# Causal attention with a cumulative bias, then two feed-forward layers: the last 64 queries of two heads in one score tile

## The chip, the cores and the metric

The kernel runs on one core of one Trainium2 chip. The metric is the device time of one execution in microseconds (us); three timed executions of the kernel before gave 1062.91, 1063.27 and 1064.26 us, the median being 1063.27 us. TensorE (PE) multiplies matrices into PSUM, VectorE (DVE), ScalarE (ACT) and GpSimd (POOL) do the elementwise work, and SyncE (SP) issues the DMAs.

## The reference

```python
# q, k, v: (4, 8, 576, 64), s: (4, 8, 576)
scores = (1/sqrt(64)) * q @ k.T
cum = cumsum(max(s, 0), axis=-1)
scores = where(causal, -1e9, scores + min(-(cum_i - cum_j), 0))
attn = softmax(scores)                      # rows of 576
x = (attn @ v)                              # to (2304, 512): heads side by side
x = sigmoid(x @ w_gate) * (x @ w_val) @ w_out          # 512 -> 1536 -> 512
h = x @ w_in;  out = (h - tanh(h)) @ w_out2            # 512 -> 2048 -> 512
```

Per row of scores the term with cum_i alone cancels in the softmax, so the kernel adds only a per-key term.

## The kernel before, in words

**Stages.** Four stages follow each other: attention together with the first feed-forward layer's gate and value products (to about 484 us), the rest of these products, the product with w_out, and the second layer. The change touches the first stage alone. Most operands are kept as two fp32r halves, a high and a low one (x = xh + xl, made by ACT as a rounding copy and by POOL or DVE as a subtraction), so that a product takes two or three fp32r matmuls.

**Units and steps.** A unit is one head of one batch and one query group: group 0 has queries 0 to 255, group 1 has queries 256 to 575 with all 576 keys. All 32 units of group 0 come first, then the 32 of group 1. A unit is walked in steps, one for a tile of 128 queries (`steps`, L258): t = 0, 1 in group 0 and t = 2, 3, 4 in group 1, with 384, 512 and 576 keys. The tile t = 4 is queries 448 to 575, of which t = 3 has done the first 64 already; the scores are made for all 128, and only rows 64 to 127 are transposed and kept (L423 to L428).

**One iteration of the loop** (L612 to L695) is a software pipeline written out by hand; each engine gets its instructions in this order. In iteration i: DVE adds 1e-9 to the sum of step i-1 (`eps`), makes the biased scores and row minima of step i out of PSUM (`ttr`, L391), takes the reciprocal for step i-1 and, for t = 2, also normalises it (`norm`, L416); for t = 3 and 4 POOL normalises (L414). ACT copies the transposed probabilities of step i-2 out of PSUM and DVE makes their low halves (`evac`, L446 and L447); ACT does the exponentials of step i (L398); POOL masks the diagonal block of the bias row to be used two steps later (`mask`, L349). Then come the finishing of a head's output (`xsum` L494 and L495, in the next iteration `xsplit` L503 and L504), the tanh or gating of the feed-forward group before (`moe_post`), and one entry of `parts`: the splitting of a coming head's keys (ACT L318, POOL L319), queries (ACT L322, POOL L323) or values (L336, L337). PE's order in iteration i is: scores of step i+1 (`qk`), one feed-forward group of 12 matmuls (`moe`), the transposes of step i-1 (`tr`, into PSUM bank 6), after a head's last step the product with v (`pv`, bank 7), and further feed-forward groups.

**How many feed-forward groups** an iteration gets is k = ceil(groups waiting / iterations left), with `left` set when a batch of heads begins (L617). When the last head of a batch is finished, 24 groups for the 24 products of that batch and group are queued. In the 24 iterations of a batch one group each is the rule; in each later batch the iteration in which a new queue is filled has k = 0 (the old one is just used up), and in the middle two batches the one behind it has k = 2. The first batch of group 1 works on what group 0 left, with 256 columns a matmul; later ones have 320.

**Names.** The probabilities of one head lie in `pth`, `ptl` (one buffer, five key blocks by 320 queries); `cbc` is the bias row of a head, loaded as a broadcast over 128 partitions; `sp` is the score tile; `kh`, `kl`, `qs` are the split keys and queries; `xp`, `xh`, `xl` a pair of heads' output and its halves.

Of the kernel before, what the change touches and what calls it, by code (L numbers as in the profile page):

```python
# [25 lines left out]
MASK = -(2.0 ** 33)  # L26
CO = {0: 0, 1: 128, 2: 0, 3: 384, 4: 896}
CW = 1184
LN = 1
# [34 lines left out]
def attention_moe_moe2(ctx: ExitStack, tc: tile.TileContext, kqT, v, s, wg, wv, wo, win, wo2, out):  # L64
# [181 lines left out]
    a_right = ExitStack()  # L246
    pt = a_right.enter_context(tc.tile_pool(name="pt", bufs=1, side="right"))
# [3 lines left out]
    cv = a_right.enter_context(tc.tile_pool(name="cv", bufs=2, side="right"))  # L251

    make_identity(nc, ident)
    NPT = 1
    pts = [[]]
# [24 lines left out]
    def load_vc(u):  # L280
        if u >= len(units):
            return
        b, h, q0, kw, qw, nj = shape(u)
        d = U_[u]
        if u >= N32:
            d["v"] = ld.tile([128, 5, D], F, tag="v", name="vraw")[:, :nj]
        else:
# [20 lines left out]
    def split_kq(u):  # L308
        if u < N32 or u >= len(units):
            return  # L310
        b, h, q0, kw, qw, nj = shape(u)
        d = U_[u]
        d["kh"] = kh = at.tile([128, S], R, tag="kh", name="kh", bufs=NK)[:, :kw]
        d["kl"] = kl = at.tile([128, S], R, tag="kl", name="kl", bufs=NK)[:, :kw]
        d["qs"] = qs = at.tile([128, 320], R, tag="qs", name="qs", bufs=NK)[:, :qw]

        def part_k():
            ACT.activation(out=kh, in_=d["k"], func=AF.Copy)  # L318
            POOL.tensor_tensor(out=kl, in0=d["k"], in1=kh.bitcast(F), op=ALU.subtract)  # L319

        def part_q():
            ACT.activation(out=qs, in_=d["q"], func=AF.Copy)  # L322
            POOL.tensor_tensor(out=qs[64:128], in0=d["q"][64:128], in1=qs[64:128].bitcast(F), op=ALU.subtract)  # L323
# [20 lines left out]
    def mask(i):  # L344
        if 2 * N32 <= i < len(steps):
            u, t = steps[i]
            e = CO[t] + (288 if t == 4 else width(t))
            c = U_[u]["c"][:, e - 128:e]
            POOL.affine_select(out=c, in_=c, pattern=[[-1, 128]], base=0, channel_multiplier=1,  # L349
                               compare_op=ALU.is_ge, fill=MASK)  # L350

    def qk(i):
# [7 lines left out]
        if u < N32:  # L360
# [5 lines left out]
            return  # L366
        cuts = [(0, max(w, 256))] if t < 4 else [(0, 288), (288, 576)]
        T_[i] = {"qk": []}
        for c0, c1 in cuts:
            ps = bank(3 + nqk[0] % 3, [128, c1 - c0])  # L370
            nqk[0] += 1
            PE.matmul(ps, d["qs"][:, o:o + 128], d["kh"][:, c0:c1], start=True, stop=False)  # L372
            PE.matmul(ps, d["qs"][:, o:o + 128], d["kl"][:, c0:c1], start=False, stop=True)
            T_[i]["qk"].append((ps, c0, min(c1, w)))

    def ttr(i):
# [10 lines left out]
        for k, (ps, c0, c1) in enumerate(e.pop("qk")):  # L387
            init, acc = acc, e["nm"][:, k:k + 1]
            o = CO[t] if t < 4 else CO[4] - 288 if c0 else CO[3]
            cum_t = zero[:, 0:w] if u < N32 else U_[u]["c"][:, o + c0:o + c1]  # L390
            DVE.tensor_tensor_reduce(out=sp[:, c0:c1], in0=ps[:, 0:c1 - c0], in1=cum_t, scale=-0.125,  # L391
# [26 lines left out]
    def tr(i):  # L418
# [3 lines left out]
        e = T_[i]  # L422
        p0 = 64 if t == 4 else 0  # L423
        e["n"] = n = 128 - p0
        blocks = [128 * j for j in range(t + 1)] if t < 4 else [0, 128, 256, 384, 448]
        ps = bank(2 if i < TR2 and i % 2 else 6, [128, len(blocks), n])
        for j, c in enumerate(blocks):
            PE.transpose(ps[:, j, :], e["sp"][p0:128, c:c + 128], ident[p0:128, p0:128])  # L428
        e["tr"] = ps

    def evac(i):
# [4 lines left out]
        e = T_.pop(i)  # L436
        n = e["n"]
        if u < N32:
            if t == 0:
                U_[u]["p"] = at.tile([128, 3, 128], F, tag="vs", name="p32")  # L440
            ACT.activation(out=U_[u]["p"][:, t:2 * t + 1], in_=e["tr"], func=AF.Copy)
            return
        ph, pl = pts[u % NPT]
        o = Q0[t] - GRP[G][0] + (64 if t == 4 else 0)
        js = slice(0, t + 1) if G else slice(0, 3 * t + 1, 3)
        ACT.activation(out=ph[:, js, o:o + n], in_=e["tr"], func=AF.Copy)  # L446
        DVE.tensor_tensor(out=pl[:, js, o:o + n], in0=e["tr"], in1=ph[:, js, o:o + n].bitcast(F), op=ALU.subtract)  # L447

# [3 lines left out]
    def pv(u):  # L452
# [4 lines left out]
        if u < N32:  # L457
# [4 lines left out]
            return ps  # L462
        ph, pl = pts[u % NPT]
        jobs = [(0, 0, 0), (1, 3, 0)] if G == 0 else [(0, 0, 0), (1, 1, 0), (2, 2, 0), (3, 3, 64), (4, 4, 64)]
# [88 lines left out]
    for u in range(2):  # L553
# [5 lines left out]
    identb, upper = consts[:, 256:320].bitcast(BF), consts[:, 320:384].bitcast(BF)  # L559
    some = consts[:, 1024:1152].bitcast(BF)  # L560
    DVE.memset(zt, 0.0)
    DVE.memset(consts[:, 512:768], 0.37)
    DVE.tensor_tensor_scan(out=consts[:, 768:1024], data0=consts[:, 512:768], data1=consts[:, 512:768], initial=0.0,
                           op0=ALU.add, op1=ALU.add)
    ACT.activation(out=some, in_=consts[:, 768:1024], func=AF.Copy)
    POOL.memset(consts[:, 0:512], 0.0)
# [37 lines left out]
    lag = [2 if j < 2 * N32 else LN for j in range(n)]  # L604
    xq, xs = [], []

# [4 lines left out]

    for i in range(n + LN + 1):  # L612
# [25 lines left out]
        if i < n:  # L638
            exp(i)
            mask(i + 2)  # L640
        while xs:
            xu = xs.pop(0)
# [5 lines left out]
        while xq:  # L648
# [4 lines left out]
            else:  # L653
                xs.append(xu)
        if first:
            if vparts:
                vparts.pop(0)()
            split_kq(u + KA)
            split_v(u + 1)
# [19 lines left out]
        for e in es:  # L679
            if e == n - 1 or steps[e][0] != steps[e + 1][0]:  # L680
                xq.append((steps[e][0], pv(steps[e][0])))
        if i < n and t == 4 and vparts:
            vparts.pop(0)()
        for j in range(1, k):
# [3 lines left out]
        if i == 2 * N32:  # L688
            cvt.finish(len(cq) - 1)
            for p in "hl":  # L690
                pts[0].append(pt.tile([128, 5, 320], R, tag=f"pt{p}", name=f"pt{p}0"))
                POOL.memset(pts[0][-1][:, 3].bitcast(F), 0.0)
        if 2 * N32 + 4 <= i < 2 * N32 + 8:
            p, c = divmod(i - 2 * N32 - 4, 2)
            POOL.memset(pts[0][p][:, 3 * c + 1:c + 3 + c].bitcast(F), 0.0)  # L695
    for x in xq:
# [308 lines left out]
```

## Time and profile before

| | us |
|---|---|
| median of three timed executions | 1063.27 |
| the profiled execution, timed | 1064.41 |
| its span, first to last instruction | 1062.3 |
| PE busy (share of the span) | 1031.9 (97%) |
| DVE busy | 662.1 (62%) |
| ACT busy | 524.9 (49%) |
| POOL busy | 465.4 (44%) |

The span leaves 2.1 us of the profiled execution's time outside. Busy shares are averages over stages that differ; a matmul's row is longer than its slot on PE, as matmuls are pipelined, so the slots are read from where the next one starts. "Idle before" names what ended an engine's idle time. The granted clock is 1.00 where TensorE runs at 2.4 GHz and 0.50 where it runs at 1.2 GHz.

### The profile page before, as it was taken

The page shows a single profiled execution, that of the slowest core. Times are in us where ns is not written, and L with a number is a line of the kernel's source. Part 1 is how long each engine was busy: PE and PEld are TensorE (multiplying, and loading weights), DVE is VectorE, ACT ScalarE, POOL GpSimd, SP SyncE. Part 2 cuts the span into 40 slices and gives each one's busy share as a digit, 9 for nine tenths or more (in the row PEclk, how much of TensorE's full clock was granted, in tenths as well). Part 3 has the DMA queues.
Part 4 walks back from the last instruction along what each step waited for, and adds up shares of the span by engine and source line. Part 5 has one row for each costly group of instructions (what it writes and reads, how often), then busy time and mean ns, then how long its engine had stood idle before and what let it go on. Part 6 is the DMA issues. An engine that isn't in the chain of part 4 may idle for free.

```text
span 1062.3 us, 20117 instructions
## 1 busy us (share of the span) xinstructions
PE 1031.9 (97%) x6892; PEld 954.2 (90%) x6892; DVE 662.1 (62%) x1563; ACT 524.9 (49%) x1193; POOL 465.4 (44%) x606
## 2 busy tenths in 40 slices
PE   7888999999999999999999999999999999999998
PEld 5787999998999999999988888988888889999997
DVE  6686566777677777665523443265655245888875
ACT  6775566766666566653523333244443333334333
POOL 4676455667566666642400010046465212454442
PEclk9999999999999999999999999999999999999999
DMA  7774456757664565515553342256597687444433
GB/s 210 219 243 107 113 139 177 200 155 171 144 174 135 159 173 159 134 51 188 172 173 117 120 117 78 99 183 221 202 326 283 222 312 259 139 117 142 142 99 100
DMA packets 111142, 177.12 MB, mean 167 GB/s; under 512 B 16000, under 2 KB 75392, under 8 KB 109760
## 3 DMA queue, kind: packets, MB, share of 16 engines
q1 hardware_dynamic: 111040, 175.85, 54.6%
q8 instruction: 54, 0.88, 0.4%
q14 instruction: 48, 0.39, 0.1%
HBM read 128.79 MB, written 47.00 MB: 165 GB/s over the span
## 4 chain that ended last, share of the span: by engine, by line
PE 86%; DVE 5%; issue 3%; DMA 2%; ACT 2%; POOL 1%; SPq 1%; DVEq 0%; POOLq 0%; ACTq 0%
PE bank L526 8%; PE bank L527 8%; PE bank L530 8%; PE bank L819 6%; PE bank L818 6%; PE bank L822 6%; PE bank L958 5%; PE bank L957 5%; PE bank L956 5%; PE bank L467 5%; PE bank L777 5%; PE bank L776 5%; PE bank L780 5%; PE bank L428 4%; PE bank L372 2%
## 5 line engine op out<-in xcount | busy, mean ns | idle before, releaser
L958 PE MATMUL bank<-wo,sl 128*128 128x256 f32 x504 | 142.5, 283 | 0.8 <-DVE sl L867 0.8
L956 PE MATMUL bank<-wo,sh 128*128 128x256 f32 x504 | 141.8, 281 | 0.3 <-ACT sh L865 0.3
L957 PE MATMUL bank<-wo,sh 128*128 128x256 f32 x504 | 141.7, 281 | 0.0
L446 ACT ACTIVATE pth<-bank 128x512 fp32r<-128x512 f32 (+2 forms) x128 | 59.5, 465 | 143.4 <-PE bank L467 84.0
L819 PE MATMUL bank<-y,ring 128*128 128x512 f32 (+1 forms) x320 | 115.8, 368 | 0.0
L818 PE MATMUL bank<-y,ring 128*128 128x512 f32 (+1 forms) x320 | 115.7, 368 | 0.0
L447 DVE TENSOR_TENSOR ptl<-bank,pth 128x512 fp32r<-128x512 f32 (+2 forms) x128 | 66.7, 521 | 67.9 <-ACT pth L446 38.5
L825 DVE TENSOR_TENSOR th<-bank,th 128x512 f32<-128x512 f32 (+1 forms) x80 | 50.2, 635 | 92.6 <-ACT th L824 90.5
L114 POOL TENSOR_TENSOR ring<-tmp,ring 128x512 fp32r<-128x512 f32 x16 | 22.5, 1406 | 187.6 <-ACT ring L124 167.4
L398 ACT ACTIVATE sp<-sp,nm 128x576 f32<-128x576 f32 (+2 forms) x160 | 95.6, 597 | 7.4 <-DVE nm L391 7.4
L958 PEld LDWEIGHTS bank<-wo,sl 128*128 128x128 f32 x504 | 95.2, 189 | 1.8 <-DVE sl L867 1.2
L862 POOL TENSOR_TENSOR s<-g 128x256 f32<-128x256 f32 (+1 forms) x40 | 34.3, 858 | 141.4 <-DMA g<-h 133.8
L956 PEld LDWEIGHTS bank<-wo,sh 128*128 128x128 f32 x504 | 95.2, 189 | 0.5 <-ACT sh L865 0.5
L957 PEld LDWEIGHTS bank<-wo,sh 128*128 128x128 f32 x504 | 95.2, 189 | 0.0
L733 DVE TENSOR_TENSOR gl<-g,gh 128x512 fp32r<-128x512 f32 (+1 forms) x60 | 37.8, 637 | 84.5 <-PE bank L780 63.5
L428 PE MATMUL bank<-ident,sp 128*128 128x128 f32 (+1 forms) x480 | 74.1, 262 | 16.5 <-POOL sp L414 7.2
L824 ACT ACTIVATE th<-bank 128x512 f32<-128x512 f32 (+1 forms) x80 | 43.7, 551 | 80.4 <-PE bank L822 76.3
L732 ACT ACTIVATE gh<-g 128x512 fp32r<-128x512 f32 (+1 forms) x60 | 35.1, 591 | 90.2 <-PE bank L777 83.3
L822 PE MATMUL bank<-y,ring 128*128 128x512 f32 (+1 forms) x320 | 78.7, 368 | 0.0
L414 POOL TENSOR_SCALAR sp<-sp,r 128x512 f32<-128x512 f32 (+1 forms) x90 | 57.1, 635 | 47.3 <-DVE r L407 40.7
L428 PEld LDWEIGHTS bank<-ident,sp 128*128 128x128 f32 (+1 forms) x480 | 51.7, 139 | 28.4 <-POOL sp L414 11.1
L865 ACT ACTIVATE sh<-g 128x768 fp32r<-128x768 f32 (+1 forms) x40 | 31.3, 781 | 88.4 <-PE bank L957 58.4
(376 smaller groups left out, 3199.5 us busy)
## 6 DMA issues: line engine op xcount, KB each, us to landing
h<-th SPq DMA_DIRECT2D x64, 256.0 KB, 2.8
kq<-in_kq SPq DMA_DIRECT2D x32, 448.0 KB, 3.8
raw<-in_wo SPq DMA_DIRECT2D x28, 512.0 KB, 5.2
g<-g SPq DMA_DIRECT2D x48, 256.0 KB, 2.7
g<-h SPq DMA_DIRECT2D x72, 128.0 KB, 2.2
w<-wst SPq DMA_DIRECT2D x5, 1792.0 KB, 6.0
wo<-w SPq DMA_DIRECT2D x5, 1792.0 KB, 9.1
cbc<-cum SPq DMA_DIRECT2D x32, 256.0 KB, 5.4
```

The costliest lines, as they stand in the source:

```text
L398: ACT.activation(out=e["sp"], in_=e["sp"], func=AF.Exp, scale=-1.0, bias=e["m"], accum_out=e["sum"])
L428: PE.transpose(ps[:, j, :], e["sp"][p0:128, c:c + 128], ident[p0:128, p0:128])
L447: DVE.tensor_tensor(out=pl[:, js, o:o + n], in0=e["tr"], in1=ph[:, js, o:o + n].bitcast(F), op=ALU.subtract)
L526: PE.matmul(ps, wh[:, c], xh[:, k], start=(k == 0), stop=False)
L527: PE.matmul(ps, wl[:, c], xh[:, k], start=False, stop=False)
L530: PE.matmul(ps, wh[:, c], xl[:, k], start=False, stop=(k == KD - 1))
L818: PE.matmul(ps, wh[:, c], yh[k], start=(k == 0), stop=False)
L819: PE.matmul(ps, wl[:, c], yh[k], start=False, stop=False)
L822: PE.matmul(ps, wh[:, c], yl[k], start=False, stop=(k == KD - 1))
L956: PE.matmul(o, sh[:, g, c], w[:, 0, f], start=(p == 0 and t == 0), stop=False)
L957: PE.matmul(o, sh[:, g, c], w[:, 1, f], start=False, stop=False)
L958: PE.matmul(o, sl[:, g, c], w[:, 0, f], start=False, stop=(p == MP - 1 and t == nt - 1))
```

## The change

Heads are taken in pairs in group 1. The even head has the steps t = 2, 3 and the odd head t = 2, 3, 4: five steps a pair. The one t = 4 step holds the last 64 queries of the even head in rows 0 to 63 of its score tile and those of the odd head in rows 64 to 127. For that the split queries `qs` get 64 columns of zeros, behind the even head's last 64 queries and ahead of the odd head's, and four matmuls per half of the keys accumulate into one PSUM tile. The bias of that tile is a row of its own, `c4`, with one head in each half of the partitions. The five key blocks are transposed whole (128 by 128), four into bank 6 and the fifth into one of the banks of the scores. The probabilities are held for two heads; the two products with v stand in consecutive iterations. The splits of keys, queries and values, and the loads, are spread anew over the five iterations. The odd head's queries are split in two pieces.

```diff
@@ constants, steps
-CO = {0: 0, 1: 128, 2: 0, 3: 384, 4: 896}
-CW = 1184
+CO = {0: 0, 1: 128, 2: 0, 3: 384}
+CW = 896
-    steps = [(u, t) for u, (b, G, h) in enumerate(units) for t in GRP[G][2]]
+    steps = [(u, t) for u, (b, G, h) in enumerate(units) for t in GRP[G][2] if t < 4 or h % 2]
@@ split_kq, split_v
+        if not Q_:
+            for j in range(4):
+                Q_.append(at.tile([128, 384], R, tag="qs", name=f"qs{j}", bufs=4))
+                POOL.memset(Q_[j][:, 320 - 64 * (j % 2):384 - 64 * (j % 2)].bitcast(F), 0.0)
+        d["qs"] = qs = Q_[u % 4]
+        pieces = ((0, 256, 0), (256, 320, 320)) if qw > 256 and h % 2 else ((0, qw, 0),)
...
-        vparts.append(part_v)
+        (vparts if qw == 256 else parts).append(part_v)
@@ qk
+        if t == 4:
+            for c0, c1 in ((0, 288), (288, 576)):
+                ps = bank(3 + nqk[0] % 3, [128, c1 - c0])
+                nqk[0] += 1
+                for a, x in enumerate((U_[u - 1], d)):
+                    PE.matmul(ps, x["qs"][:, 256:384], x["kh"][:, c0:c1], start=(a == 0), stop=False)
+                    PE.matmul(ps, x["qs"][:, 256:384], x["kl"][:, c0:c1], start=False, stop=(a == 1))
+                T_[i]["qk"].append((ps, c0, c1))
+            return
@@ tr, evac
-            PE.transpose(ps[:, j, :], e["sp"][p0:128, c:c + 128], ident[p0:128, p0:128])
-        e["tr"] = ps
+            PE.transpose(e["tr"][j // 4][:, j % 4, :], e["sp"][:, c:c + 128], ident)
+        if t == 4:
+            for k, src in enumerate(e["tr"]):
+                src = src.rearrange("p j (a q) -> p a j q", a=2)
+                ph, pl = (P_[x][:, :, 4 * k:4 + k, 256:320] for x in range(2))
+                ACT.activation(out=ph, in_=src, func=AF.Copy)
+                DVE.tensor_tensor(out=pl, in0=src, in1=ph.bitcast(F), op=ALU.subtract)
+            return
@@ the loop
-            left = (16 if G == 0 else 24) + LN + 2 + (2 if u + H == len(units) else u + H == 4 * H)
+            left = (16 if G == 0 else 21) + LN + 2 + (2 if u + H == len(units) else u + H == 4 * H)
+        elif i < n and G == 1:
+            s = t - 2 if h % 2 == 0 else t
+            if s in (0, 4):
+                split_kq(u + KA)
+                load_kq(u + KA + 1)
+            if s in (0, 2):
+                load_c(u + 2)
+            if s == 0:
+                load_c4(u + 1)
+            if s in (2, 3):
+                split_v(u + s - 3)
+            if s in (3, 4):
+                load_v(u + s - 2)
-        for _ in range(2 if first and G == 0 else 1):
+        for _ in range(2 if first and G == 0 else 1 + (t == 4)):
             if parts:
                 parts.pop(0)()
...
-                xq.append((steps[e][0], pv(steps[e][0])))
-        if i < n and t == 4 and vparts:
-            vparts.pop(0)()
+            if steps[e][1] in (1, 4):
+                pvs.extend(range(steps[e][0] - steps[e][1] // 4, steps[e][0] + 1))
+        if pvs:
+            xu = pvs.pop(0)
+            xq.append((xu, pv(xu)))
...
+                P_.append(pp.tile([128, 2, 5, 320], R, name=f"pt{p}"))
+                POOL.memset(P_[-1][:, :, 3].bitcast(F), 0.0)
+        if 2 * N32 + 4 <= i < 2 * N32 + 6:
+            POOL.memset(P_[i - 2 * N32 - 4][:, :, 4].bitcast(F), 0.0)
```

Not shown: the warm-up constants shrink from 256 to 128 columns, `mask` covers `c4` in two 64 by 64 pieces, and the loads are written as functions of their own.

On PE before, the step t = 4 of one head: its predecessor's transposes do not stand here, only its own and the scores of the next tile; this piece comes twice a pair (sp is the score tile, ident the identity).

```order
L530 MATMUL bank_5408<-xl,w17h 128x320 x4
L428 MATMUL bank_5421<-ident,sp 128x64 x5
L372 MATMUL bank_5445<-kh,qs 128x288
L373 MATMUL bank_5445<-kl,qs 128x288
L372 MATMUL bank_5448<-kh,qs 128x288
L373 MATMUL bank_5448<-kl,qs 128x288
L526 MATMUL bank_5451<-xh,w08h 128x320
```

On PE now, the scores of the pair's one t = 4 tile, which begin the iteration of the odd head's t = 3 (qs_1266 is the even head, qs_1268 the odd one).

```order
L514 MATMUL bank_5114<-ptl,vs 128x256
L401 MATMUL bank_5156<-kh,qs_1266 128x288
L402 MATMUL bank_5156<-kl,qs_1266 128x288
L401 MATMUL bank_5156<-kh,qs_1268 128x288
L402 MATMUL bank_5156<-kl,qs_1268 128x288
L401 MATMUL bank_5161<-kh,qs_1266 128x288
L402 MATMUL bank_5161<-kl,qs_1266 128x288
L401 MATMUL bank_5161<-kh,qs_1268 128x288
L402 MATMUL bank_5161<-kl,qs_1268 128x288
L573 MATMUL bank_5166<-xh,w16h 128x320
```

The number of score matmuls of the pair is unchanged; they stand together, behind a product with v and no longer behind transposes.

On POOL before, one unit of group 1 and the start of the next: between the normalising of t = 4 (L414, 576 keys) and that of t = 3 (512 keys) of the next unit stand the low halves of the output (L504), of the keys (L319) and of the queries (L323).

```order
L414 TENSOR_SCALAR sp<-sp,r 128x512
L349 AFFINE_SELECT cbc<-cbc 128x128
L337 TENSOR_TENSOR vs<-vraw,vs 128x5x64
L414 TENSOR_SCALAR sp<-sp,r 128x576
L349 AFFINE_SELECT cbc<-cbc 128x128
L504 TENSOR_TENSOR xl<-xp,xh 128x320
L319 TENSOR_TENSOR kl<-kq,kh 128x576
L349 AFFINE_SELECT cbc<-cbc 128x128
L323 TENSOR_TENSOR qs<-kq,qs 64x320
L414 TENSOR_SCALAR sp<-sp,r 128x512
```

On POOL now, around the same place (L453 normalises, L551 is the output's low half, L341 the keys', L347 the queries').

```order
L361 TENSOR_TENSOR vs<-vraw,vs 128x5x64
L453 TENSOR_SCALAR sp<-sp,r 128x512
L377 AFFINE_SELECT cbc<-cbc 128x128
L551 TENSOR_TENSOR xl<-xp,xh 128x320
L341 TENSOR_TENSOR kl<-kq,kh 128x576
L347 TENSOR_TENSOR qs_1268<-kq,qs_1268 64x256
L347 TENSOR_TENSOR qs_1268<-kq,qs_1268 64x64
L453 TENSOR_SCALAR sp<-sp,r 128x576
L377 AFFINE_SELECT cbc<-cbc 128x128
L341 TENSOR_TENSOR kl<-kq,kh 128x576
```

The output's, the keys' and both pieces of the queries' low halves now stand between the normalising of t = 3 and that of t = 4, whose steps follow each other directly.

On ACT now, the iteration of t = 4 and the start of the next (L493 copies transposes out, L437 is the exponential, L550 the output's high half, L340 the keys', L345 the queries').

```order
L493 ACTIVATE pth<-bank_5179 128x3x128
L437 ACTIVATE sp,sum<-sp,nm 128x576
L550 ACTIVATE xh<-xp 128x320
L340 ACTIVATE kh<-kq 128x576
L345 ACTIVATE qs_1272<-kq 128x256
L345 ACTIVATE qs_1272<-kq 128x64
L493 ACTIVATE pth<-bank_5230 128x4x128
```

The high halves that POOL's four subtractions start from come behind the copy of the odd head's t = 2 and the exponential of t = 4.

## Rows read from the trace of the kernel before

**Rows 1.** The page's chain that ended last, shares of the span.
```profile
PE 86%; DVE 5%; issue 3%; DMA 2%; ACT 2%; POOL 1%; SPq 1%; DVEq 0%; POOLq 0%; ACTq 0%
```

**Rows 2.** Busy us by engine (PE, PEld, DVE, ACT, POOL), then clock: two heads.
```profile
300.00:319.00 19.00, 19.00 (x135) 18.28 (x135) 13.89 (x42) 12.28 (x32) 12.01 (x18) 1.00 0.58 157
```

**Rows 3.** The chain in order of time: start us, us, what; one unit.
```profile
304.54 0.33 PE bank L428 x3
304.86 1.35 PE bank L467 x10
306.21 0.18 PE bank L372
...
306.57 0.14 PE bank L526
...
308.32 0.44 PE bank L428 x4
...
309.21 0.15 PE bank L526
...
310.97 0.45 PE bank L428 x5
311.42 0.33 PE bank L372
...
312.15 0.14 PE bank L526
```

**Rows 4.** PE in order of time, group 1: start, us, instruction, [idle before].
```profile
261.90 0.49 PE L428 MATMUL bank<-ident,sp 64*128 64x64 f32 x5 [1.10 <-POOL sp L414]
```

**Rows 5.** ACT in order of time, 305 to 309 us.
```profile
305.70 0.49 ACT L446 ACTIVATE pth<-bank 128x384 fp32r<-128x384 f32 x1 [1.74 <-PE bank L467]
306.08 0.77 ACT L398 ACTIVATE sp<-sp,nm 128x576 f32<-128x576 f32 x1
...
306.97 0.43 ACT L494 ACTIVATE xtmp<-bank 64x320 f32<-64x320 f32 x1
...
308.85 0.60 ACT L446 ACTIVATE pth<-bank 128x512 fp32r<-128x512 f32 x1 [1.09 <-PE bank L428]
```

**Rows 6.** ACT and POOL in order of time, 261 to 263 us.
```profile
261.05 0.74 POOL L414 TENSOR_SCALAR sp<-sp,r 128x576 f32<-128x576 f32 x1
261.53 0.46 ACT L503 ACTIVATE xh<-xp 128x320 fp32r<-128x320 f32 x1
...
262.07 0.88 POOL L504 TENSOR_TENSOR xl<-xp,xh 128x320 fp32r<-128x320 f32 x1
...
262.90 1.44 POOL L319 TENSOR_TENSOR kl<-kq,kh 128x576 fp32r<-128x576 f32 x1
```

**Rows 7.** POOL's groups by line and shape: busy us, mean ns, idle before.
```profile
L323 POOL TENSOR_TENSOR qs<-kq,qs 64x256 fp32r<-64x256 f32 x16 | 11.8, 737 | 1.3
L337 POOL TENSOR_TENSOR vs<-vraw,vs 128x128 fp32r<-128x128 f32 x16 | 7.3, 459 | 36.3 <-ACT vs L336 36.3
```

**Rows 8.** DVE's normalising of t = 2: min/median/max ns, 265 to 475 us.
```profile
L416 DVE TENSOR_SCALAR sp<-sp,r x22: 420/1624/1637, 273.5 to 471.8; 128x384 f32<-128x384 f32 x22
```

**Rows 9.** POOL in order of time: a mask behind a key split.
```profile
303.32 0.43 POOL L349 TENSOR_SCALAR_AFFINE_SELECT cbc<-cbc 128x128 f32<-128x128 f32 x1
...
306.11 0.29 POOL L349 TENSOR_SCALAR_AFFINE_SELECT cbc<-cbc 128x128 f32<-128x128 f32 x1
```

**Rows 10.** PE in order of time near 98 us.
```profile
97.45 0.33 PE L428 MATMUL bank<-ident,sp 128*128 128x128 f32 x1 [1.55 <-DVE ptl L447]
98.34 0.58 PE L467 MATMUL bank<-pth,vs 128*128 128x256 f32 x1 [0.56 <-DVE xl L483]
```

**Rows 11.** Stretches there: as rows 2.
```profile
95.00:100.00 5.00, 2.90 (x16) 2.45 (x15) 2.35 (x9) 3.08 (x12) 2.40 (x5) 0.84 0.39 91
100.00:105.00 5.00, 5.00 (x37) 5.00 (x37) 2.78 (x13) 1.97 (x8) 3.36 (x7) 0.82 0.25 74
```

**Rows 12.** The zeroing of the probabilities' halves: min/median/max ns.
```profile
L692 POOL MEMSET pth<- x1: 516/516/516, 92.1 to 92.1; 128x320 f32 x1
```

More of the change, by code (lines that the diff above doesn't have):

```diff
@@ L321, in part_q @@
         def part_q():
-            ACT.activation(out=qs, in_=d["q"], func=AF.Copy)
-            POOL.tensor_tensor(out=qs[64:128], in0=d["q"][64:128], in1=qs[64:128].bitcast(F), op=ALU.subtract)
+            for c0, c1, o in pieces:
+                ACT.activation(out=qs[:, o:o + c1 - c0], in_=d["q"][:, c0:c1], func=AF.Copy)
+                low = qs[64:128, o:o + c1 - c0]
+                POOL.tensor_tensor(out=low, in0=d["q"][64:128, c0:c1], in1=low.bitcast(F), op=ALU.subtract)
         parts.extend([part_k, part_q])
@@ L337, in part_v, with mask @@
             POOL.tensor_tensor(out=vs[:, :, 1 - a, :], in0=d["v"], in1=vs[:, :, a, :].bitcast(F), op=ALU.subtract)
-        vparts.append(part_v)
+        (vparts if qw == 256 else parts).append(part_v)
     T_ = {}
     nqk = [0]
-    def mask(i):
-        if 2 * N32 <= i < len(steps):
+    def mask(i, last=False):
+        if 2 * N32 <= i < len(steps) and last == (steps[i][1] == 4):
             u, t = steps[i]
[L347 to L350, printed above, removed]
+            if last:
+                cs = [U_[u]["c4"][64 * a:64 * a + 64, S - 64:S] for a in range(2)]
+            else:
+                e = CO[t] + width(t)
+                cs = [U_[u]["c"][:, e - 128:e]]
+            for c in cs:
+                POOL.affine_select(out=c, in_=c, pattern=[[-1, c.shape[1]]], base=0, channel_multiplier=1,
+                                   compare_op=ALU.is_ge, fill=MASK)
     def qk(i):
@@ L436, in evac @@
         e = T_.pop(i)
-        n = e["n"]
+        tr0 = e["tr"][0]
         if u < N32:
@@ L462, in pv @@
             return ps
-        ph, pl = pts[u % NPT]
+        ph, pl = (P_[x][:, u % 2] for x in range(2))
         jobs = [(0, 0, 0), (1, 3, 0)] if G == 0 else [(0, 0, 0), (1, 1, 0), (2, 2, 0), (3, 3, 64), (4, 4, 64)]
@@ L559, in attention_moe_moe2 @@
     identb, upper = consts[:, 256:320].bitcast(BF), consts[:, 320:384].bitcast(BF)
-    some = consts[:, 1024:1152].bitcast(BF)
+    some = consts[:, 768:896].bitcast(BF)
     DVE.memset(zt, 0.0)
-    DVE.memset(consts[:, 512:768], 0.37)
-    DVE.tensor_tensor_scan(out=consts[:, 768:1024], data0=consts[:, 512:768], data1=consts[:, 512:768], initial=0.0,
+    DVE.memset(consts[:, 512:640], 0.37)
+    DVE.tensor_tensor_scan(out=consts[:, 640:768], data0=consts[:, 512:640], data1=consts[:, 512:640], initial=0.0,
                            op0=ALU.add, op1=ALU.add)
-    ACT.activation(out=some, in_=consts[:, 768:1024], func=AF.Copy)
+    for c in (0, 128):
+        ACT.activation(out=some[:, c:c + 128], in_=consts[:, 640:768], func=AF.Copy)
     POOL.memset(consts[:, 0:512], 0.0)
@@ L604, in attention_moe_moe2 @@
     lag = [2 if j < 2 * N32 else LN for j in range(n)]
-    xq, xs = [], []
+    xq, xs, pvs = [], [], []
     def whole(xu):
@@ L610, in whole @@
             mq.extend((gg, m, w) for m in range(M1) for w in range(2))
-    for i in range(n + LN + 1):
+    for i in range(n + LN + 2):
         u, t = steps[i] if i < n else (None, None)
@@ L640, in attention_moe_moe2 @@
             mask(i + 2)
+            mask(i + 1, True)
         while xs:
@@ L654, in attention_moe_moe2 @@
                 xs.append(xu)
-        if first:
-            if vparts:
-                vparts.pop(0)()
+        if first and vparts:
+            vparts.pop(0)()
+        if first and G == 0:
             split_kq(u + KA)
-            split_v(u + 1)
+            if u + 1 < 4 * H:
+                split_v(u + 1)
             if u + KA + 1 >= N32:
@@ L689, in attention_moe_moe2 @@
             cvt.finish(len(cq) - 1)
+            while cvt.rest:
+                cvt.low()
+            c_right.close()
+            pp = a_right.enter_context(tc.tile_pool(name="pp", bufs=1, side="right"))
             for p in "hl":
[L691 to L695, printed above, removed]
+                P_.append(pp.tile([128, 2, 5, 320], R, name=f"pt{p}"))
+                POOL.memset(P_[-1][:, :, 3].bitcast(F), 0.0)
+        if 2 * N32 + 4 <= i < 2 * N32 + 6:
+            POOL.memset(P_[i - 2 * N32 - 4][:, :, 4].bitcast(F), 0.0)
     for x in xq:
```

69 lines of the change are left out of this document (42 added, 27 removed).

## The prediction

> **What bounds the kernel now.** I read the chain that ended last first: 86% of the span is PE's [rows 1]. Then the stage that the change touches. Two heads of group 1 take some 18.8 us; in 19 us there PE is busy all the time and POOL, the least loaded of the others, 12.0 us [rows 2]. The chain of one unit in order of time holds nothing but PE [rows 3], so what PE saves there is saved, as long as no other engine becomes late. The only idle time of PE there beyond some 0.2 us is 1.10 us before the transposes, three times (261.90 us is the first, the others follow a batch apart): the iterations without a feed-forward group [rows 4].
>
> I write E2, E3, O2, O3, T4 for the pair's five steps: the even head's t = 2, 3, the odd head's, and the common t = 4.
>
> **What PE saves.** From the start of the five 64-column transposes to the first feed-forward matmul are 310.97 to 312.15, 1.18 us a head, 2.36 us a pair [rows 3]. In it the first score matmul behind the transposes takes 0.33 us, the other three 0.40 together, 0.13 each. Now a pair has five transposes of 128 columns at 0.44 / 4 = 0.11 us [rows 3], 0.55, and eight score matmuls behind a product with v at 0.13, 1.07: 1.62 us. Saved: 0.74 us a pair, 11.8 us in 16 pairs. The products with v and the feed-forward groups are as many as before. Bounds: at 0.09 us a transpose (0.45 / 5, the 64-column rate) 13.4 us; with the slow first matmul kept, 0.2 us a pair less, 8.6 us. I take 11.8, since the 128-column row is the same operation.
>
> The row shows 64-column transposes almost as dear as 128-column ones (0.09 against 0.11 us). A rule of the Trainium skill speaks against this saving (TensorE: Matmul & The Clock Gate, section "Back-to-back issue gap"): a matmul's slot goes by its moving columns, about 60 cycles at 64 and 134 at 128, so five wide transposes would cost slightly more than ten narrow ones. By it the saving would be about 0.35 us a pair, an estimate, and the sum 6 us higher. The trace disagrees.
>
> **What the other engines lose and gain.** One of two 576-key steps goes with its minima, exponential, reciprocal and normalising, and none of these was on the path [rows 3]. But 24 feed-forward groups a batch now fall on 20 iterations, mostly one in each, so a pair with five groups gives the others less PE time to hide under. Where the order on POOL matters is T4 and the E2 behind it.
>
> **The new wait: the transposes of T4.** They stand on PE at the end of E2's iteration and need POOL's normalising of T4. In POOL's queue the low halves of the output, of the odd head's keys and of both query pieces stand between the normalising of O3 and it. Before, such a run lay between the normalisings of t = 4 and of the next t = 3, two iterations apart, with a DVE step between. I count both ways from one moment, the end of O2's transposes on PE.
>
> POOL's way: ACT begins to copy these transposes 0.10 us later (308.75, the transposes' end in rows 3, to 308.85 in rows 5), is free after 0.38 (305.70 to 306.08), after the exponential of 576 keys another 0.89 (to 306.97) [rows 5]; then xh, and POOL's xl 0.54 behind its start (261.53 to 262.07), next on POOL 0.83 later (to 262.90), the keys 1.44 [rows 6], 256 query columns 0.74, 64 query columns an estimate of 0.32 (128 columns take 0.46, 128 more cost 0.28 [rows 7]), the normalising 0.74, and PE 0.11 behind its end (261.05 + 0.74 to 261.90) [rows 4, 6]. Sum: 6.1 us.
>
> PE's way with one group an iteration: scores of 384 keys 0.36, a group 1.75, four transposes and scores of 512 keys 0.89, a group 1.75 [rows 3]: 4.75 us. PE waits 1.35 us. With the 256-column groups of the first batch a group is 1.40 (estimate, by columns), PE's way 4.05, the wait 2.05.
>
> Walking the rule for k through the 80 steps gives for the 16 T4s: six with 320 columns and one group (1.35 each, 8.1); three with 256 columns (2.05, 6.15); the first, with two groups, 0.65; two with two groups of 320, none; the last, behind which no keys are split, none; and three without a group. There the O3 transposes wait for bank 6 as before, 1.10 us with a 512-column copy ahead [rows 4], I take 1.0 with 384; then PE reaches T4's transposes after 0.36 + 1.0 + 0.89 + 1.75 = 4.0 us and waits 2.1: 3.1 us each, 9.3. In all 24.2 us of waits, where there were 3.3. Net: 24.2 - 3.3 - 11.8 = 9.1 us longer.
>
> Queued behind the waiting transposes on PE is all of E3; nothing makes up for it, since the next pair's count starts again from PE. Bounds for each wait: without the 64-column piece 0.32 less, with 0.46 for it 0.14 more; over 12 places -3.9 to +1.7.
>
> **Two costs on top.** DVE's normalising of E2 becomes ready while POOL works through that run. Such an operation takes 0.42 us alone and 1.62 in most cases [rows 8], and a POOL mask that it met took 0.43 instead of 0.29 us [rows 9]. If it slips in ahead of T4's normalising, POOL pays 0.14 us, over 12 places 1.7 us, which I take; ends 0 and 12 x 0.42 = 5.0. The Trainium skill (SBUF — State Buffer, section "SBUF: two separate sides") has VectorE and GpSimd share a port pair that the first comer holds for its whole instruction; by it the price would be the whole 0.42. The one row at hand shows a third of that.
>
> The clock: where PE stood idle for 1.55 and 0.56 us within 3 us [rows 10], the granted clock was 0.84 and 0.82 over the next ten [rows 11], a fall to 1.2 GHz that cost 5 x 0.16 + 5 x 0.18 = 1.7 us; a single 1.10 us did nothing [rows 2, 4]. The three places without a group now have 1.0 and 2.1 us close together. I take one fall in two, 2.5 us; ends 0, and 10 us if the three first-batch waits of 2.05 fall too.
>
> **What I cost at nothing.** The odd head's product with v must wait until the even head's result is read from bank 7: ACT's read began 0.76 us behind the product's end (306.21 to 306.97) [rows 3, 5] and DVE's sum about as long as it behind; PE has scores, a group and transposes in between, over 2.6 us. The zeroings: a 320-column one takes 0.52 us [rows 12]; four small ones near 76 us and 640 columns more near 92 us cost POOL at most 3 us, hidden under feed-forward groups there, while the low half of a weight no longer waits behind two of them (0.9 us). I take 0 within -0.9 and 3. The shorter warm-up constants end before the first scores, which wait for a DMA: 0.
>
> **The sum.** 9.1 + 1.7 + 2.5 = 13.3 us on the profiled execution's 1064.4 (span 1062.3 and 2.1 outside): 1077.7. The median lies 1.1 us below that execution, so I forecast 1077 us; with the bounds, 1068 to 1086.
>
> **Rivals.** (1) Faster: POOL keeps up, because xh or the keys come earlier than my count has them, and T4's transposes never wait. For it: POOL is busy in 12 of 19 us only, and loses one normalising of 0.74 us a pair [rows 2, 6]. Against it: the order on POOL and ACT, in which nothing can pass. Time: saved 11.8, and three waits of 1.0 for three of 1.10, 12.1 us: 1064.4 - 12.1 - 1.1 = 1051. It decides as soon as POOL's way is under 4.05 us, 2 us less than I count.
> (2) No change: POOL's way is about 0.75 us shorter than counted, 12 places give back 9 us and the clock does not fall: 1063 to 1065.
> (3) Still slower: the clock falls in all six long waits and DVE's operation costs its whole 0.42: 9.1 + 5.0 + 10 = 24 us, 1087.
> (4) The skill's transpose rule holds: 6 us on top of the forecast, 1083.
>
> **How the numbers follow.** Forecast 0.72, rival 1 0.13, rival 2 0.08, rival 3 0.05, rival 4 0.02. About 0.2% (2.1 us) is what a measurement of this kernel can tell from no change. Slower: forecast, rivals 3 and 4 and half of rival 2, 0.83. Same: half of rival 2, 0.04. Faster: 0.13. The range from 1062 to 1086 leaves out rival 1 and the upper part of rival 3.
>
> **What would show it.** Right: in the changed profile PE idles before the transposes (L469) with POOL's normalising (L453) as releaser a dozen times, 1.3 to 2.1 us each, every fourth pair worse, and on POOL the run xl, kl, two query pieces, normalising stands without a gap; a quiet pair has about 17.6 us, the last product with v comes near 497 us instead of 484, and all behind it is as long as before. The transposes of 128 columns keep 0.11 us. Wrong: PE waits there for nothing, or DVE or a DMA is named instead; or the granted clock stays at 1.00 and the waits are half as long.

## The result, and the profile after

The changed kernel takes 1076.94 us (median of 4 runs, 1071.99 to 1078.57) where the kernel before took 1063.76 (1062.91 to 1065.2). The ratio is 1.0115, with an interval of 1.008 to 1.015: slower, by 13 us, 0.1 us from the forecast of 1077.

The profiled execution is the quickest of the four, 1071.99 us, with a span of 1070.2 us and a mean granted clock of 0.998. The other three have 0.992 or 0.993 and are 4.8 to 6.6 us longer. Much of what follows is read from the quick one, so the clock has a point of its own below.

The chain that ended last, in the profile after, answers [rows 1]:

```profile
PE 77%; POOL 6%; issue 5%; DVE 4%; ACT 4%; DMA 3%; SPq 1%; POOLq 0%; DVEq 0%; ACTq 0%
```

PE's share fell from 86 to 77%, POOL's rose from 1 to 6%. PE's waits by releaser in the profile after, from 180 to 495 us (us in total, times, longest):

```profile
PE bank L469 <- POOL sp L453: 18.6, 12, 1.9
PE bank L469 <- DVE ptl L494: 2.7, 3, 0.9
```

The same view of the kernel before, as far as its transposes go:

```profile
PE bank L428 <- DVE ptl L447: 2.2, 2, 1.1
PE bank L428 <- POOL sp L414: 1.1, 1, 1.1
...
PE bank L428 <- DVE sum L402: 0.7, 4, 0.2
```

In the profile after, the first row is the new wait: the transposes of T4 for POOL's normalising, twelve times. The second is the old one of 1.10 us in three iterations [rows 4], which is left.

PE in order of time in the profile after, one pair's T4 (start us, us, instruction, [idle before]); it answers [rows 3]:

```profile
303.70 0.49 PE L469 MATMUL bank<-ident,sp 128*128 128x128 f32 x3
303.95 0.43 PE L409 MATMUL bank<-kh,qs 128*128 128x384 f32 x1
...
304.39 0.31 PE L573 MATMUL bank<-xh,w07h 128*128 128x320 f32 x1
...
306.14 0.60 PE L469 MATMUL bank<-ident,sp 128*128 128x128 f32 x4
...
308.22 0.75 PE L577 MATMUL bank<-xl,w17h 128*128 128x320 f32 x4
310.17 0.77 PE L469 MATMUL bank<-ident,sp 128*128 128x128 f32 x5 [1.20 <-POOL sp L453]
310.69 0.43 PE L409 MATMUL bank<-kh,qs 128*128 128x384 f32 x1
```

ACT in the same profile over the same stretch, and then POOL; they answer [rows 5, 6]:

```profile
304.23 0.49 ACT L493 ACTIVATE pth<-bank 128x384 fp32r<-128x384 f32 x1 [1.92 <-PE bank L469]
304.61 0.77 ACT L437 ACTIVATE sp<-sp,nm 128x576 f32<-128x576 f32 x1
...
305.37 0.46 ACT L550 ACTIVATE xh<-xp 128x320 fp32r<-128x320 f32 x1
...
305.92 0.87 POOL L551 TENSOR_TENSOR xl<-xp,xh 128x320 fp32r<-128x320 f32 x1 [1.10 <-ACT xh L550]
306.74 1.44 POOL L341 TENSOR_TENSOR kl<-kq,kh 128x576 fp32r<-128x576 f32 x1
308.26 1.02 POOL L347 TENSOR_TENSOR qs<-kq,qs 64x256 fp32r<-64x256 f32 x2
309.37 0.74 POOL L453 TENSOR_SCALAR sp<-sp,r 128x576 f32<-128x576 f32 x1
```

The transposes of O2 are over at 303.95, where the next row starts. POOL's way from there is a chain of starts: ACT's copy (+0.28), the exponential (+0.38), xh (+0.76), POOL's xl (+0.55), the keys (+0.82), the two query pieces (+1.52), the normalising (+1.11), PE's transposes (+0.80): 6.22 us. PE's way ends 1.20 us before 310.17, at 308.97: 5.02 us. POOL waits for nothing from xl to the normalising, and 1.10 us ahead of xl: it works only 11.12 of 19 us here, and PE waits for it all the same. The same 19 us by windows, as [rows 2]:

```profile
300.00:319.00 19.00, 17.80 (x127) 17.32 (x127) 11.13 (x36) 12.39 (x33) 11.12 (x18) 1.00 0.53 155
```

Behind the stage, PE in the profile before and in the one after, at the first of a group's matmuls that both have:

```profile
493.83 0.41 PE L526 MATMUL bank<-xh,w11h 128*128 128x320 f32 x1 [1.00 <-ACT th L539]
```

```profile
500.79 0.41 PE L573 MATMUL bank<-xh,w11h 128*128 128x320 f32 x1 [1.64 <-ACT th L586]
```

It comes 6.96 us later. The waits are 18.6 + 2.7, where there were 3.3 and four short ones of 0.7 together, so 17.3 more, and 0.6 more at this place: 17.9 us. So the change saved some 11 us of PE's own time here, where 11.8 had been forecast. From here to the end of the span another 0.9 us are lost, 0.71 of them in one wait for DVE at 904 us (L1025). That is the 7.9 us by which the spans differ.

### The profile page after: what moved, and what is told of

It is laid out like the page before. It is cut to its first block, busy times and chain, and to the rows that moved or that the text cites. A ratio compares the mean times of both kernels' runs of the same rounds, so it can differ in the third digit from the quotient of the medians.

```text
span 1070.2 us, 19673 instructions
## 1 busy us (share of the span) xinstructions
PE 1021.3 (95%) x6812; PEld 949.6 (89%) x6812; DVE 621.1 (58%) x1467; ACT 511.3 (48%) x1178; POOL 456.1 (43%) x608
## 4 chain that ended last, share of the span: by engine, by line
PE 77%; POOL 6%; issue 5%; DVE 4%; ACT 4%; DMA 3%; SPq 1%; POOLq 0%; DVEq 0%; ACTq 0%
PE bank L573 7%; PE bank L577 7%; PE bank L574 7%; PE bank L886 6%; PE bank L885 6%; PE bank L889 6%; PE bank L847 5%; PE bank L843 5%; PE bank L844 5%; PE bank L1025 5%; PE bank L1024 4%; PE bank L1023 4%; PE bank L514 4%; PE bank L469 3%; POOL sp L453 2%
## 5 line engine op out<-in xcount | busy, mean ns | idle before, releaser
L1025 PE MATMUL bank<-wo,sl 128*128 128x256 f32 x504 | 142.7, 283 | 1.8 <-DVE sl L934 1.5
L493 ACT ACTIVATE pth<-bank 128x384 fp32r<-128x384 f32 (+1 forms) x96 | 45.4, 473 | 124.9 <-PE bank L469 98.0
L469 PE MATMUL bank<-ident,sp 128*128 128x128 f32 x400 | 69.2, 278 | 33.4 <-POOL sp L453 25.2
L494 DVE TENSOR_TENSOR ptl<-bank,pth 128x384 fp32r<-128x384 f32 (+1 forms) x96 | 51.4, 535 | 83.7 <-ACT pth L493 83.5
L1025 PEld LDWEIGHTS bank<-wo,sl 128*128 128x128 f32 x504 | 95.2, 189 | 3.0 <-DVE sl L934 1.9
L929 POOL TENSOR_TENSOR s<-g 128x256 f32<-128x256 f32 (+1 forms) x40 | 37.0, 926 | 139.9 <-DMA g<-h 132.9
L437 ACT ACTIVATE sp<-sp,nm 128x128 f32<-128x128 f32 (+4 forms) x144 | 83.5, 580 | 9.1 <-DVE nm L430 9.1
L469 PEld LDWEIGHTS bank<-ident,sp 128*128 128x128 f32 x400 | 48.6, 141 | 40.7 <-POOL sp L453 30.2
L361 POOL TENSOR_TENSOR vs<-vraw,vs 128x320 fp32r<-128x320 f32 (+1 forms) x48 | 35.4, 738 | 100.0 <-ACT vs L360 93.1
L589 DVE SCALAR_TENSOR_TENSOR gt<-th,bank 128x256 f32<-128x256 f32 (+1 forms) x96 | 43.2, 450 | 53.4 <-PE bank L577 37.2
```

The costliest lines, as they stand in the source:

```text
L437: ACT.activation(out=e["sp"], in_=e["sp"], func=AF.Exp, scale=-1.0, bias=e["m"], accum_out=e["sum"])
L469: PE.transpose(e["tr"][j // 4][:, j % 4, :], e["sp"][:, c:c + 128], ident)
L1025: PE.matmul(o, sl[:, g, c], w[:, 0, f], start=False, stop=(p == MP - 1 and t == nt - 1))
```

## The experiments

The kernel before ran beside each; a ratio is to it. All edits but the last are to the changed kernel.

**The changed kernel again.**

> The changed kernel itself once more, as the base of the runs beside it. Theory: PE waits some 18.6 us in twelve places for POOL's normalising of the common t = 4 tile, and the granted clock falls behind one to three of the three iterations without a feed-forward group, 1.7 us each, so single executions differ: 1071 to 1079 us, the slower ones with the lower mean clock (0.992 against 0.998). Rival (the time lies in the paired tile's own work on PE): the executions agree within 0.3% as those of the kernel before do.

Measured: 1075.94 us (1072.04 to 1082.07, 6 runs), ratio 1.0127 [1.0104, 1.015]. The result holds, and the rival is out: the executions do not agree within 0.3%. The reason that was expected for their spread is not shown: in the profile, of the slowest, the clock fell behind one of the three iterations, as in the quick one, and four times elsewhere (the point on the clock has the rows). The six executions go by their clock: 0.998, 0.996, 0.995, 0.993, 0.992, 0.990 with 1072.04, 1074.70, 1076.12, 1075.76, 1077.77, 1082.07 us.

**The splits put elsewhere in the pair.** The odd head's keys are split at O3, its queries in the next E2 behind the normalising of T4; T4 splits nothing. The loads of keys and queries move with them.

```diff
-            if s in (0, 4):
+            if s in (2, 3):
+                split_v(u + s - 3)
+            if s in (0, 3):
                 split_kq(u + KA)
+            if s in (1, 4):
                 load_kq(u + KA + 1)
...
-        for _ in range(2 if first and G == 0 else 1 + (t == 4)):
+        for _ in range(2 if first and G == 0 else (2, 1, 1, 2, 0)[s] if i < n and G else 1):
```

> The changed kernel with only the place of the splits moved: the odd head's keys are split in the iteration of its t = 3, its queries behind the normalising of t = 4, so that POOL has nothing but a mask and one low half between the two normalisings. Theory: the twelve waits for POOL go, the three waits of 0.9 us for the bank stay; 1072 - 18.6 = 1053 us without clock falls, and the saving of 11.7 us on PE becomes visible. Rival 1 (five steps a pair are too few to hide the other engines, wherever the splits stand): another engine takes POOL's place as releaser and the time stays above 1065. Rival 2 (the paired tile itself costs PE time): no change, 1072 or more.

Measured: 1055.76 us (1052.54 to 1059.1), ratio 0.9934 [0.9915, 0.9953]: 20 us below the changed kernel that ran beside it, and faster than before. PE's waits from 180 to 495 us:

```profile
PE bank L469 <- POOL sp L453: 2.7, 3, 0.9
PE bank L573 <- ACT th L586: 2.2, 1, 2.2
PE bank L469 <- DVE sum L441: 1.2, 1, 1.2
PE bank L409 <- POOL qs L347: 0.3, 1, 0.3
```

Of 21.3 us of waits at L469, 3.9 are left, and none of these is at T4: all stand before the four transposes of O3, three of them in the iterations without a feed-forward group. So T4's waits come from where the splits stand, and not from what the change computes. This edit moves copies on ACT along with POOL's subtractions; the doubled subtraction and the normalising on DVE, further down, leave ACT's queue as it is.

**The groups dealt out differently**, over 22 places and not 21, so that no iteration of the first three batches goes without one: alone, and together with the splits moved.

```diff
-            left = (16 if G == 0 else 21) + LN + 2 + (2 if u + H == len(units) else u + H == 4 * H)
+            left = (16 if G == 0 else 22) + LN + 2 + (2 if u + H == len(units) else u + H == 4 * H)
```

> The changed kernel with only the groups spread further, the splits as they are. Theory: the bank waits (2.7 us) go, the three waits of 1.86 become about 1.24 to 1.55, two T4 iterations that had two groups now have one and wait 1.24 each, 19.6 us of waits instead of 21.3, so 1070 us where the clock does not fall; and as no wait of 0.9 and one of 1.9 stand close together any more, the clock falls behind none of them and all executions agree within 0.3%, mean clock 0.998 or more. Rival (the clock falls wherever PE waits 1.2 us or more): the spread of the executions stays, 1071 to 1079.

> The same, and the feed-forward groups spread one iteration further (left counted from 22 instead of 21), so that no iteration is without a group. Theory: the three bank waits of 0.9 us go as well and the clock stays up: 1050 us, all executions within 0.3%. Rival: the waits come back elsewhere, 1053 or more.

Measured: alone 1070.19 us (1066.4 to 1074.14), ratio 1.0071 [1.0051, 1.0091]; together 1054.57 (1052.05 to 1056.57), ratio 0.9918 [0.9904, 0.9933]. Alone, PE still waits twelve times for POOL, 17.2 us, and the three bank waits are gone. A group more in the iteration shortens T4's wait there only from 1.86 to the 1.2 to 1.5 of its neighbours. The 1070 us were met, but not the reason: without the pairs of waits close together the clock was to stay up and the executions to agree within 0.3%, and they spread by 0.7%. The one fall in this profile ahead of its end follows a wait of 1.87 us with no other within 10 us of it, the second of the first batch (windows as [rows 2]):

```profile
232.50:236.50 4.00, 3.85 (x19) 3.85 (x20) 1.96 (x7) 2.10 (x6) 2.63 (x5) 0.57 0.88 201
```

Together, 1050 us and 0.3% were expected, and 1054.57 and 0.4% came out. The bank waits are gone, and in the stage the profile has 0.9 us before one step's transposes and 0.6 for queries, so the rival's number came without its reason; the mean clock, 0.993 to 1.000, is not up in all executions.

**One piece of POOL's run taken out**: the odd head's queries are split in the next E2.

```diff
-        for _ in range(2 if first and G == 0 else 1 + (t == 4)):
+        for _ in range(2 if first and G == 0 else 1 + (i < n and G == 1 and t == 2 and h % 2 == 0)):
```

> The odd head's query split leaves T4 and is done in the next E2, so POOL's run ahead of T4's normalising loses the 256-column and the 64-column piece (0.74 + 0.32 us by the sum of the prediction). Theory (PE waits for POOL's run in order): the six waits of 1.24 us shrink to about 0.2, the three of 1.87 (256-column groups) and the three of 1.86 (no group) to about 0.8; 12.6 us less than the changed kernel's 1076, some 1063 us. Rival A (the waits are set by ACT, whose exponential and copies come too late for POOL, so that POOL's run is not what counts): ACT loses the two query copies as well, but the waits shrink by less than 0.5 us each, 1070 us or more. Rival B (DVE's normalising of E2 holds the port and makes POOL late): the waits stay, 1076 us.

Measured: 1064.12 us (1061.57 to 1066.49, 10 runs), ratio 1.0005 [0.9991, 1.0019]. PE's waits from 180 to 495 us:

```profile
PE bank L469 <- POOL sp L453: 4.0, 6, 0.7
PE bank L409 <- POOL qs L347: 2.8, 9, 0.4
PE bank L469 <- DVE ptl L494: 2.7, 3, 0.9
PE bank L573 <- ACT th L586: 2.6, 1, 2.6
```

The six waits of 1.2 us vanish, the six of 1.87 shrink to 0.67: by 1.2 us each, for a run 1.1 us shorter. Rivals A and B are out: A allowed less than 0.5 us, B nothing. The expectation did not have the second row: the queries, now split later, are themselves waited for nine times, 0.3 us each.

**One piece doubled**: the odd head's key subtraction twice.

```diff
-            POOL.tensor_tensor(out=kl, in0=d["k"], in1=kh.bitcast(F), op=ALU.subtract)
+            for _ in range(1 + (u >= 4 * H + 2 and h % 2)):
+                POOL.tensor_tensor(out=kl, in0=d["k"], in1=kh.bitcast(F), op=ALU.subtract)
```

> POOL subtracts the odd head's keys twice in T4 (the second time gives the same numbers), nothing else is changed. Theory: each of the 12 waits for T4's normalising grows by the 1.4 us of one subtraction (16.8 us), and the T4s with two groups, which did not wait, begin to, by up to 1 us each: 1076 + 18 to 20, some 1095 us, more where the clock falls. Rival A (ACT or DVE sets the waits and POOL has slack of its own): less than half of that, under 1085 us.

Measured: 1112.58 us (1104.48 to 1114.22), ratio 1.0451 [1.0408, 1.0495]. PE's waits from 180 to 540 us (lines are one further on):

```profile
PE bank L470 <- POOL sp L454: 38.0, 13, 3.4
```

19.4 us more of waits: twelve are longer by 1.5, as the theory said, and of the three T4s with two groups, which were to begin to wait, one does, by 1.46. Together with the run before, POOL's run moves the wait one for one in both directions. But the time grew by 36 us, nearly twice as much, and 1095 us was expected: the mean clock is 0.975 to 0.984 here, some 0.015 lower, which is 16 us of 1090.

**The normalising of t = 4 on DVE**, so that it doesn't stand in POOL's queue at all.

```diff
 def NORM(G, t):
-    return "pool" if t > 2 else "dve"
+    return "pool" if t == 3 else "dve"
```

> The normalising of t = 4 goes to DVE, so that it stands no longer behind POOL's run; POOL keeps the splits and t = 3. Theory: the waits of PE for POOL at L469 go, and waits for DVE in their place stay below 0.5 us; the time is the changed kernel's 1076 less about 15 us, some 1061 us. Rival (DVE beside POOL's key subtraction takes 1.6 instead of 0.4 us, and POOL in turn is held up): PE waits for DVE at the same place by 1 us or so, 1070 us or more.

Measured: 1053.25 us (1051.98 to 1053.61), ratio 0.9906 [0.9891, 0.9922]. PE's waits from 180 to 495 us:

```profile
PE bank L469 <- DVE ptl L494: 2.7, 3, 0.9
PE bank L573 <- ACT th L586: 1.3, 1, 1.3
PE bank L409 <- POOL qs L347: 0.4, 1, 0.4
```

No wait for POOL's normalising, and none for DVE's in its place. The waits sum to 4.4 us, where the kernel before has 5.0 (3.3, 0.7 and 1.0), so the saving shows almost by itself. The group's matmul of 493.83 us starts here 11.8 us earlier, of which 0.6 are waits and 11.2 the saving:

```profile
482.04 0.41 PE L573 MATMUL bank<-xh,w11h 128*128 128x320 f32 x1 [1.30 <-ACT th L586]
```

A quiet pair says the same. From one T4's transposes to the next, in this profile:

```profile
304.62 0.71 PE L469 MATMUL bank<-ident,sp 128*128 128x128 f32 x5
320.93 0.71 PE L469 MATMUL bank<-ident,sp 128*128 128x128 f32 x5
```

That is 16.31 us with five feed-forward groups; two heads before took 18.77 (292.13 to 310.90) with six. A group is 1.76 us (302.86 to 304.62), so 0.70 us a pair are saved, 11.2 in 16 pairs. The expectation of 1061 was 8 us too high: it counted 15 of the 18.6 us that the waits return, and not the clock, which is 0.997 or 0.998 in all four executions.

**The same, with the groups over 22 places.**

> The normalising of t = 4 on DVE, and the feed-forward groups dealt out over one step more, so that no iteration in the first three batches is without a group. Theory: the three waits of 0.91 us for DVE's copy of bank 6 go too, and no wait of PE beyond 0.5 us is left between 180 us and the last product with v: 2 to 3 us less than with the DVE normalising alone, some 1051 us. Rival (a group later in the next batch, or behind the last batch, costs what the waits cost): 1053 us, the same.

Measured: 1049.58 us (1047.44 to 1050.87), ratio 0.986 [0.9843, 0.9877]: the best version, 14 us under the kernel before. The three bank waits are gone; 0.9 at the end of the stage and twice 0.37 for queries are what PE still waits in it. Its chain:

```profile
PE 87%; DVE 3%; DMA 3%; issue 2%; ACT 2%; POOL 1%; SPq 1%; DVEq 0%; POOLq 0%; ACTq 0%
```

**The kernel before with the normalising of t = 4 on DVE**, the control: the same edit, without the change.

> The kernel before with the normalising of t = 4 on DVE. Theory: the kernel before never waits for POOL at t = 4, so nothing is gained, 1063 us plus or minus 1; what the DVE normalising is worth is worth it only where the change put POOL's run ahead of it. Rival (DVE's place is better for reasons of its own, less traffic beside the key subtraction for example): 1055 us, and then the changed kernel with it on DVE shows no gain of the change.

Measured: 1063.66 us (1062.36 to 1066.57), ratio 1.0001 [0.9991, 1.0012]. DVE is no better place as such; it is one only where POOL's run stands ahead of the normalising.

## Why the prediction was right, point by point

**What PE saves: right in kind, a little too large.** Five transposes take 0.52 us (310.17 to 310.69), 0.104 each, where the forecast had 0.11 from [rows 3]; without a wait ahead they take 0.46 (304.62 to 305.08 with the normalising on DVE), 0.09 each, and the 64-column ones before took 0.09 too (310.90 to 311.35). The eight score matmuls behind the product with v start 0.12 to 0.14 us apart, as forecast. The whole was to be 11.8 us and is 11.0 to 11.2 by the two profiles. The first scores behind T4's transposes take 0.08 us more than behind a product with v, which the forecast had only in its bounds, as the slow first matmul.

The table of the Trainium skill that the prediction drew on (TensorE: Matmul & The Clock Gate, section "Back-to-back issue gap") gives the gaps of isolated matmuls, and says itself that in a stream of weight loads and matmuls both set the spacing. Every transpose here has a weight load (400 of each in the profile after), and at 0.09 us for 64 columns and for 128 the table does not fit them. With it the saving would have been some 6 us, an estimate of the prediction; rival 4 is out.

**The new wait: right mechanism, each term a little too large.** POOL's way was to be 6.1 us and is 6.22; PE's 4.75, and it is 5.02, since a group's last matmuls end 0.17 us later than the sum of starts has it and the first scores take 0.08 more; POOL's is longer by less. So 1.20 to 1.28 for 1.35, six times; 1.87 for 2.05, three times; and 1.86 for 2.1 at the three places without a group, with 0.91 for 1.0 ahead of each. The first T4, priced at 0.65, does not wait: that step failed, though the doubled subtraction shows it just on the edge (+1.44 there gave 1.46). In all 21.3 us for 24.2; net of 4.0 before and some 11 saved, 6.3 us for 9.1.

**DVE in front of the normalising, 1.7 us: not there.** T4's normalising on POOL takes 0.75 us on the mean, as in [rows 6], and stands right behind the queries. DVE's normalising of E2 now falls beside the query pieces and not beside the key subtraction. Its minimum, median and maximum from 265 to 475 us, in the profile after, answer [rows 8]:

```profile
L455 DVE TENSOR_SCALAR sp<-sp,r x22: 420/508/837, 266.2 to 473.3; 128x384 f32<-128x384 f32 x22
```

0.51 us where it took 1.62. DVE is quicker by the change, and off the path either way.

**The clock, 2.5 us: seen once in three places, and most of its price is elsewhere.** Behind the last place without a group, granted clocks in the profile after:

```profile
422.00:423.00 1.00, 0.00 (x0) 0.00 (x0) 0.96 (x4) 0.18 (x1) 0.94 (x2) 1.00 0.07 16
423.00:424.00 1.00, 0.16 (x1) 0.16 (x2) 0.16 (x1) 0.00 (x0) 0.96 (x3) 0.99 0.20 18
424.00:425.00 1.00, 1.00 (x6) 1.00 (x6) 0.00 (x0) 0.10 (x1) 1.00 (x2) 0.50 0.65 201
...
427.00:428.00 1.00, 1.00 (x7) 1.00 (x7) 0.00 (x0) 0.04 (x1) 0.81 (x1) 0.80 0.80 236
```

One fall at the three places, to 1.2 GHz for some 3.4 us, costs 1.7 us, where the forecast, one fall in two, had 2.5. The one of [rows 11] isn't in this profile, so the two cancel in the spans. But the median execution has a mean of 0.992 to 0.993, 0.005 to 0.006 less than this one, and is 5 us longer: so much of the 13 us is the clock's. The second profile of the changed kernel (mean 0.990, span 10.1 us longer) has five falls:

```profile
18.00:26.00 8.00, 6.78 (x28) 5.81 (x29) 3.39 (x16) 3.33 (x13) 2.53 (x5) 0.57 0.56 150
79.00:84.00 5.00, 4.51 (x20) 4.03 (x21) 4.17 (x11) 3.14 (x10) 3.58 (x7) 0.66 0.48 166
349.00:354.00 5.00, 4.44 (x21) 4.45 (x22) 1.15 (x3) 2.15 (x6) 3.24 (x5) 0.66 0.69 188
506.00:511.00 5.00, 4.90 (x23) 4.90 (x24) 3.97 (x7) 3.47 (x7) 2.82 (x2) 0.66 0.54 164
912.00:917.00 5.00, 4.29 (x23) 4.29 (x24) 4.74 (x7) 2.14 (x3) 0.10 (x1) 0.66 0.44 126
```

Only the one at 349 us stands behind a place without a group, so there too it is one of three. The others are two ahead of 100 us, one at the end of the stage behind a wait of 3.0 us for ACT, and one at 912 us behind a wait of 2.3 us for DVE, far behind the stage that the change touches. T4's transposes start 3.8 us later than in the quick profile at the first long wait (221.10 for 217.26) and 3.95 at the last (470.12 for 466.17). So none of the 10 us between these two executions comes from the places that the forecast priced. Where the falls of the median execution stand has no profile, and why the mean is lower than before stays open.

**Where the stage ends: a miss.** The last product with v was to come near 497 us and starts at 488.3. The forecast put the whole loss ahead of it; but a group more lies behind it now (w11h follows 12.5 us later, before 10.1), 3 us of waits weren't there, and the clock's part wasn't in this execution. The quiet pair, forecast at 17.6 us, takes 17.77 (310.17 to 327.94).

So the sum, 13.3 us, came out as about 6 from the stage, 1.5 at its end and behind it, and 5 from the clock. An overcount of the waits and of DVE made up for a clock term that was half of what the clock took, and no run shows that the clock took it where the forecast had it. That the change is slower, and by which wait, was worked out; that 1077 stands so near to 1076.94 is luck. Of the rivals, (1) is what the change does once POOL's run is out of the way: 1051 was worked out for it, and 1053 was measured, and 1050 with the groups over 22 places. It lost because POOL's way is 6.2 us long; 1.1 us less of it gave back the change's whole cost and no more.

## What to carry to other kernels

An engine with time to spare can still set the pace: before merging steps, walk each in-order queue between the last thing the next step needs and what is put in front of it, and compare that way with the critical engine's way over the same stretch. Here the merge saved some 11 us and the waits took 17 to 18 back; giving one operation to an engine whose queue was free (one line) turned 1.2% slower into 0.9% faster, and evening out the filler work made it 1.4%. Where a saving on the critical engine does not show in the time, move the work that stands behind it before giving up the saving.

## What had not been expected of the hardware

**Equal idle times, different clocks.** The kernel with the doubled subtraction has two waits of PE of one length in the same batch, 3.37 us before 222.41 and 3.35 before 263.87. Stretches by windows (PE, PEld, DVE, ACT, POOL, then the clock):

```profile
219.00:223.00 4.00, 0.63 (x4) 0.59 (x4) 1.61 (x7) 0.54 (x1) 3.80 (x6) 0.79 0.12 22
223.00:227.00 4.00, 4.00 (x20) 4.00 (x19) 1.66 (x6) 2.10 (x6) 2.31 (x4) 0.50 0.93 248
260.50:264.50 4.00, 0.65 (x7) 0.63 (x7) 1.57 (x7) 0.49 (x1) 3.82 (x6) 1.00 0.13 19
264.50:268.50 4.00, 4.00 (x32) 3.90 (x31) 2.11 (x7) 3.08 (x9) 2.78 (x4) 1.00 0.67 239
```

Behind the first PE runs at 1.2 GHz, 20 matmuls in 4 us; behind the second at 2.4 GHz, 32. So a wait's price isn't read off its length, and in this kernel 19 us of added waits cost some 16 us more in clock.

**Who starts first beside the key subtraction.** In the kernel before, DVE's normalising of 384 keys that starts within 0.05 us of POOL's key subtraction takes 1.6 us [rows 8]. One of them, DVE and POOL in that profile:

```profile
283.20 1.62 DVE L416 TENSOR_SCALAR sp<-sp,r 128x384 f32<-128x384 f32 x1
```

```profile
283.16 1.44 POOL L319 TENSOR_TENSOR kl<-kq,kh 128x576 fp32r<-128x576 f32 x1
```

DVE ends 0.2 us behind the subtraction. With T4's on DVE, it starts 0.40 us ahead of the subtraction, while POOL still has the low half of the output in hand; DVE and POOL in that profile:

```profile
302.16 0.76 DVE L455 TENSOR_SCALAR sp<-sp,r 128x576 f32<-128x576 f32 x1
```

```profile
301.73 0.88 POOL L551 TENSOR_TENSOR xl<-xp,xh 128x320 fp32r<-128x320 f32 x1 [1.10 <-ACT xh L550]
302.56 1.66 POOL L341 TENSOR_TENSOR kl<-kq,kh 128x576 fp32r<-128x576 f32 x1
```

DVE ends at 302.92, 0.3 us behind the end of the row that ran before it, and the subtraction, which starts 0.36 us before DVE's end, takes 1.66 instead of 1.44. So in these rows the later one pays, and no more than the overlap. The Trainium skill has the first comer hold the shared port pair for its whole instruction (SBUF — State Buffer, section "SBUF: two separate sides"). DVE's rows agree with it. POOL's subtraction pays 0.22 of an overlap of 0.36 us, and the mask of [rows 9] had paid 0.14 of 0.26 (DVE's normalising ran to 303.58 there): 0.12 to 0.14 less than the overlap, both times. The prediction compared the mask's 0.14 with DVE's whole 0.42, but the two had not met for so long.
